# Batch 1's queries turned in full 128x128 transposes, two K^T V products joined into one stretch, and q's transposing transfers issued sooner

## The chip, the cores and the metric

One core of a Trainium2 chip. The metric is the device time of one execution in microseconds (us); a time is quoted as the median of the runs of a kernel. PE is the matrix engine, PEld its weight loads, VectorE (DVE), ScalarE (ACT) and GpSimd (POOL) the others, SP the queue that issues stores and transposing transfers.

## The reference, cut to what matters

```python
kv  = einsum('bhsd,bhse->bhde', k, v)        # 8 batches, 8 heads, 576 rows, 64 wide
out = einsum('bhsd,bhde->bhse', q, kv)       # the "scores" of the kernel
x   = out / sqrt(mean(out*out) + 1e-6) * g_norm       # -> 4608 x 512
h   = x @ w_in                                # 512 -> 2048
y   = elu(h) @ w_out                          # 2048 -> 512
```

## The kernel before: the parts concerned

Each of eight batches gives a group T of 512 rows (a ninth group takes the left-over rows). In a group, PE runs the first layer of batch T (`mm1`, eight steps i, `h_ps`), the second layer of batch T-1 (`mm2`, `o_ps`), and the attention of batch T+1 (K^T V, then scores, tiles named `at` and `se_ps`). From batch 3 on, q is turned by a transposing transfer on the SP queue. Batch 1 has no time for that and is turned on PE:

```python
def q_t_single(q_pk, qt_ps, r, p):            # 32 transposes, 64 columns of q each
    for j in range(J):
        for l in range(2):
            nc.tensor.transpose(qt_ps[l * 64 : l * 64 + 64, r, j * P : j * P + P],
                                q_pk[:, 2 * p + l, j, :], ident)
...
for j in range(J):                            # stage A: mm2 of batch 0 around batch 1
    mm2_quarter(0, j, 0)
    if j == 2: at["q"]()                      # transposes, two ACT copies to qT
for j in range(J):
    mm2_quarter(0, j, 1)
    if j == 1: at["kvu0"]()                   # first half of K^T V
    if j == 2: at["seu0"](scores); at["sq0"](); at["sum0"]()
at["inv0"](); at["mulu0"]()
for j in range(J):
    mm2(0, j, 8, 10)
    if j == 2: at["kvu1"]()                   # second half
at["seu1"](); at["sq1"](); at["sum1"]()
for j in range(J):
    mm2(0, j, 10, 12)                         # w_out's columns 10 to 12
    if j == 1: at["inv1"](); at["xu0"](scores[:, 0, :])
at["mulu1"]()
...                                           # later "xu1": transposes of x, second half
# end of a group T:  if T + 2 < NT: ahead["qd"]()     # q's transposing transfer
# start of a group:  at["landed"]()                   # GpSimd waits for that transfer
#                    fetch(T + 2)                     # then issues q, k, v of batch T+2
# in a group:        if at and i == 0: at["kv"]()     # K^T V of batch T+1
```

## Time and profile before

| | before |
|---|---|
| time, median of the first 3 runs (range) | 284.09 us (283.82 to 284.26) |
| PE busy, share of the span of 282.0 us | 98% |
| start of stage A (first `o_ps` matmul) | 28.31 us |
| stage A (to the first matmul of batch 1's first layer, which writes `at`) | 17.75 us |
| from start of A to the last five output pieces | 235.95 us |

The stages are read off PE's timeline; its starts are 0.17 us ahead of those in the chain of waits, which counts from when the engine is free. The chain and the list of PE's waits are shown in the prediction below. What it only tells is how one sees, in GpSimd's timeline, when transfers end. Columns: start, length, engine, line, operation, and in brackets how long the engine had stood idle and what ended that.

```profile
31.55 0.71 POOL L142 DMA_DIRECT2D w_out_sb<-in_moe_w_out_dram  x1 [1.80 <-DMA w_out_sb<-in_moe_w_out_dram]
33.01 0.74 POOL L104 DMA_DIRECT2D q_pk<-in_q_dram  x1 [0.74 <-DMA k_pk<-in_k_dram]
34.48 0.74 POOL L104 DMA_DIRECT2D q_pk<-in_q_dram  x1 [0.73 <-DMA v_pk<-in_v_dram]
...
37.41 0.74 POOL L118 DMA_DIRECT2D v_pk<-in_v_dram  x1 [0.68 <-DMA k_pk<-in_k_dram]
```

Each issue is held until an older transfer of the same queue has ended, so the brackets name a sequence of endings, one every 1.45 us or so.

### The profile page before, as it was taken

The numbers are of one execution on the slowest core, as the hardware profiler recorded it, in microseconds if no ns is written. First come the engines' busy times: TensorE is split into PE (matmuls) and PEld (weight loads), VectorE is DVE, ScalarE is ACT, GpSimd is POOL, SyncE is SP. The second block draws the span as 40 slices with busy tenths as digits, with TensorE's granted clock in tenths as the row PEclk, the third lists the DMA queues.
The fourth block names the chain that finished last, engine by engine and source line by source line (L and its number), as shares of the span: only waits on it lengthen the run. The fifth ranks groups of instructions, "written<-read, shape, count | busy, mean of one in ns | idle before, by whom it ended". The sixth has DMA issues, their size and how long they took to land.

```text
span 282.0 us, 5163 instructions
## 1 busy us (share of the span) xinstructions
PE 276.0 (98%) x2134; PEld 129.8 (46%) x2134; DVE 159.8 (57%) x232; ACT 153.8 (55%) x221; POOL 56.2 (20%) x98
## 2 busy tenths in 40 slices
PE   7899999999999999999999999999999999999994
PEld 3444544445444444444444444444444444444444
DVE  2559453888388546843693469445854586444400
ACT  2679546666487438533863377337923692333311
POOL 7854422143421341004110421012000000000000
PEclk9999999999999999999999999999999999999999
DMA  7999999697796696359935795455236123010122
GB/s 196 199 200 202 208 201 191 179 170 128 178 177 114 157 157 156 74 149 121 198 78 148 95 211 73 130 114 148 55 94 76 77 38 112 0 77 0 74 76 74
DMA packets 57579, 35.98 MB, mean 128 GB/s; under 512 B 32852, under 2 KB 55124, under 8 KB 57556
## 3 DMA queue, kind: packets, MB, share of 16 engines
q0 software_dynamic: 21808, 17.30, 41.2%
q1 hardware_dynamic: 35348, 17.83, 24.7%
q10 hardware_dynamic: 400, 0.52, 0.6%
q8 instruction: 16, 0.26, 0.4%
q14 instruction: 7, 0.06, 0.1%
HBM read 36.70 MB, written 9.44 MB: 164 GB/s over the span
## 4 chain that ended last, share of the span: by engine, by line
PE 94%; DMA 2%; ACT 1%; DVE 0%; issue 0%; POOL 0%; POOLq 0%
PE h_ps L467 42%; PE o_ps L514 39%; PE o_ps L924 5%; DMA v_pk<-in_v_dram 2%; PE at L174 2%; PE at L467 1%; PE bank L684 1%; PE at L201 1%; PE h_ps L684 1%; PE se_ps L201 1%; ACT r L669 0%; ACT r L672 0%; PE at L185 0%; ACT sq L663 0%; PE se_ps L413 0%
## 5 line engine op out<-in xcount | busy, mean ns | idle before, releaser
L467 PE MATMUL h_ps<-xT,w_in_sb 128*128 128x512 bf16 x536 | 125.7, 379 | 0.0
L514 PE MATMUL o_ps<-w_out_sb,gT 128*128 128x512 bf16 x512 | 120.5, 379 | 0.0
L479 ACT ACTIVATE elu_e<-h_ps 128x1024 bf16<-128x1024 f32 (+1 forms) x71 | 70.0, 995 | 80.1 <-PE h_ps L467 78.5
L467 PEld LDWEIGHTS <-w_in_sb 128*128 128x128 bf16 x552 | 52.5, 98 | 63.3 <-DVE xT L333 1.7
L514 PEld LDWEIGHTS <-gT 128*128 128x128 bf16 x512 | 49.4, 98 | 58.4
L490 DVE TENSOR_SCALAR elu_e<-elu_e 128x1024 bf16<-128x1024 bf16 (+1 forms) x75 | 31.9, 425 | 73.4 <-ACT elu_e L479 73.4
L498 DVE TENSOR_TENSOR gT<-elu_e,h_ps 128x1024 bf16<-128x1024 bf16 (+1 forms) x51 | 60.1, 1179 | 5.3
L527 ACT COPY o_sb<-o_ps 128x512 f32<-128x512 f32 x32 | 18.6, 586 | 15.5 <-PE o_ps L514 15.5
L218 DVE TENSOR_REDUCE ss<-sq 128x16 f32<-128x1024 bf16 x16 | 19.4, 1218 | 11.1 <-ACT sq L213 10.4
L485 ACT ACTIVATE elu_h<-h_ps 128x1024 bf16<-128x1024 f32 (+1 forms) x20 | 19.5, 990 | 0.0
L150 POOL COPY q_bf<-q_pk 128x512 bf16<-128x512 bf16 x24 | 14.4, 629 | 24.3 <-DMA q_pk<-in_q_dram 24.3
L498 DVE TENSOR_TENSOR gT<-elu_e,elu_h 128x1024 bf16<-128x1024 bf16 x20 | 14.2, 709 | 2.5 <-ACT elu_h L485 1.0
L924 PE MATMUL o_ps<-w_out_sb,gT 128*128 128x512 bf16 (+1 forms) x80 | 14.1, 337 | 0.0
L125 POOL COPY gate<-qT 1x1 bf16<-1x1 bf16 x6 | 1.1, 181 | 58.4 <-DMA qT<-q_bf 58.4
L104 POOL DMA_DIRECT2D q_pk<-in_q_dram x14 | 10.6, 758 | 4.5 <-issue 1.5
L229 DVE TENSOR_TENSOR xs<-at,ss 128x512 bf16<-128x512 f32 x16 | 10.2, 682 | 1.2 <-ACT ss L225 1.2
L924 PEld LDWEIGHTS <-gT 128*128 128x128 bf16 x80 | 7.8, 98 | 6.4 <-DVE gT L498 0.4
L213 ACT ACTIVATE sq<-at 128x1024 bf16<-128x1024 f32 x9 | 9.4, 1043 | 1.6 <-PE at L201 1.0
L118 POOL DMA_DIRECT2D k_pk<-in_k_dram x12 | 8.3, 690 | 3.9 <-DMA w_in_sb<-in_moe_w_in_dram 2.4
L118 POOL DMA_DIRECT2D v_pk<-in_v_dram x12 | 8.2, 683 | 3.2 <-DMA w_out_sb<-in_moe_w_out_dram 1.8
L932 ACT COPY o_last<-o_ps 128x512 f32<-128x512 f32 (+1 forms) x5 | 2.5, 500 | 10.8 <-PE o_ps L924 10.8
L174 PEld LDWEIGHTS <-k_pk 64*64 64x64 bf16 x576 | 6.4, 107 | 4.3 <-issue 4.0
(79 smaller groups left out, 140.7 us busy)
## 6 DMA issues: line engine op xcount, KB each, us to landing
out_dram<-o_sb SPq DMA_DIRECT2D x16, 512.0 KB, 3.3
q_pk<-in_q_dram POOLq DMA_DIRECT2D x14, 256.0 KB, 5.7
k_pk<-in_k_dram POOLq DMA_DIRECT2D x6, 576.0 KB, 8.3
v_pk<-in_v_dram POOLq DMA_DIRECT2D x6, 576.0 KB, 11.6
w_in_sb<-in_moe_w_in_dram POOLq DMA_DIRECT2D x5, 256.0 KB, 7.4
st_q<-in_q_dram SPq DMA_DIRECT2D x2, 512.0 KB, 4.7
w_out_sb<-in_moe_w_out_dram POOLq DMA_DIRECT2D x2, 512.0 KB, 13.9
w_out_sb<-in_moe_w_out_dram POOLq DMA_DIRECT2D x4, 256.0 KB, 12.0
```

Of the source, the lines that this page charges most:

```text
L118: nc.gpsimd.dma_start(out=raw[name, b].rearrange("p h j d -> p h (j d)")[:, hs], in_=in_[:, hs])
L150: eng.tensor_copy(out=out_, in_=in_)
L174: nc.tensor.matmul(kv_ps[l * 64 : l * 64 + 64, s, u * 64 : u * 64 + 64], lhsT=bf["k", T][rows, j, 2 * u + l, :], rhs=bf["v", T][rows, j, 2 ...
L218: nc.vector.reduce_sum(out=ss, in_=sq.rearrange("p c (h e) -> p (c h) e", h=H), axis=AX.X)
L467: nc.tensor.matmul(h_ps[a][:, cs], lhsT=w_in_sb[:, c, f * P : f * P + P], rhs=x(c, cs), start=(c == 0), stop=(c == KC - 1),)
L479: nc.scalar.activation(e[:, lo:hi, :], ps, AF.Exp)
L485: nc.scalar.activation(h[:, lo:hi, :], ps, AF.Relu)
L490: nc.vector.tensor_scalar(out=e[:, lo:hi, :], in0=e[:, lo:hi, :], scalar1=1.0, scalar2=1.0, op0=ALU.min, op1=ALU.subtract,)
L498: nc.vector.tensor_tensor(out=gT[T][:, 2 * i + lo : 2 * i + hi, :], in0=e[:, lo:hi, :], in1=h, op=ALU.add if relu else ALU.max,)
L514: nc.tensor.matmul(o_ps[T, j], lhsT=gT[T][:, f, j * P : j * P + P], rhs=w_out_sb[:, f, :], start=(f == 0), stop=(f == FC - 1),)
L527: nc.scalar.copy(o_sb[T][:, j % 2, :], o_ps.pop((T, j)))
L924: nc.tensor.matmul(ps, lhsT=gT[B][:, f, j * P : j * P + P], rhs=w_out_sb[:, f, cols], start=(f == 0), stop=(f == FC - 1),)
```

## The change

Its intent: fewer and fuller PE instructions for batch 1's q, one switch in and out of small tiles less, and enough lead for K and V of batch 7 that the joint product can run a group early. The core of the diff:

```diff
-    def q_t_single(q_pk, qt_ps, r, p):  ... 32 half-width transposes
+    def q_t_single(qb, qt_ps, p):
+        for j in range(J):
+            nc.tensor.transpose(qt_ps[:, p, j * P : j * P + P],
+                qb[:, j, 2 * p : 2 * p + 2, :].rearrange("p h d -> p (h d)"), ident)
@@ q_t
             nc.scalar.copy(qT[:, 0:2, :], qt_ps[:, 0:2, :])
-            nc.scalar.copy(qT[:, 2:4, :], qt_ps[:, 2:4, :])
+            nc.vector.tensor_copy(out=qT[:, 2:4, :], in_=qt_ps[:, 2:4, :])
@@ stage A
     load_w_out(10, 12)
+    unpack_q(1, Q, gated=False)               # four GpSimd copies, repacking q of batch 1
     load_w_out(12, 14)
@@
         mm2_quarter(0, j, 0)
-        if j == 2:
-            at["q"]()
+    at["q"]()
@@
         mm2(0, j, 8, 10)
-        if j == 2:
-            at["kvu1"]()
-    at["seu1"](); at["sq1"](); at["sum1"]()
+    at["kvu1"]()
     for j in range(J):
         mm2(0, j, 10, 12)
-        if j == 1:
+        if j == 0:
+            at["seu1"](); at["sq1"](); at["sum1"]()
+        if j == 2:
             at["inv1"](); at["xu0"](scores[:, 0, :])
@@ fetch: for batch 7 k and v ahead of q
@@ groups
-            if at and i == 0:
+            if at and i == 0 and T in (3, 4):
                 at["kv"]()
+            if i == 2 and T == 5:              # K^T V of batches 6 and 7 in one PSUM tile
+                both = at_tile(FP32).rearrange("p (s x) -> p s x", s=2)
+                ...
+            if i == 5 and T + 2 < B:           # was: at the end of the group
+                ahead["qd"]()
```

More of the change, by code (lines that the diff above doesn't have):

```diff
@@ L125, in after, with unpack_q @@
         nc.gpsimd.tensor_copy(out=gate, in_=ap)
-    def unpack_q(b, eng):
+    def unpack_q(b, eng, gated=True):
         t = raw.pop(("q", b))
@@ L130, in unpack_q @@
         for j in range(J):
-            if j == J - 1:
+            if gated and j == J - 1:
                 after(bf["v", b][0:1, 0, 0, 0:1])
@@ L180, in kv_single @@
                     )
-    def q_t_single(q_pk, qt_ps, r, p):
+    def q_t_single(qb, qt_ps, p):
         for j in range(J):
-            for l in range(2):
-                nc.tensor.transpose(
-                    qt_ps[l * 64 : l * 64 + 64, r, j * P : j * P + P],
-                    q_pk[:, 2 * p + l, j, :],
-                    ident,
-                )
+            nc.tensor.transpose(
+                qt_ps[:, p, j * P : j * P + P],
+                qb[:, j, 2 * p : 2 * p + 2, :].rearrange("p h d -> p (h d)"),
+                ident,
+            )
     def se_mm(T, h, qT, banks):
@@ L247, in q_t @@
             for p in range(NPAIR):
-                q_t_single(raw["q", T], qt_ps, p, p)
+                q_t_single(bf["q", T], qt_ps, p)
             nc.scalar.copy(qT[:, 0:2, :], qt_ps[:, 0:2, :])
-            nc.scalar.copy(qT[:, 2:4, :], qt_ps[:, 2:4, :])
+            nc.vector.tensor_copy(out=qT[:, 2:4, :], in_=qt_ps[:, 2:4, :])
         def q_dma():
@@ L355, in kv_out, with kv_in @@
             )
+        def kv_in(home):
+            st["kv"] = home
+            for u in range(2):
+                kv_single(T, home, u)
         def kv_u(u):
@@ L426, in x_u @@
             return turn
-        pieces = {"kv": kv_all, "q": q_t, "qd": q_dma, "se": se}
+        pieces = {"kv": kv_all, "kvin": kv_in, "kvout": lambda: kv_out(slice(0, 2)), "q": q_t, "qd": q_dma, "se": se}
         pieces["landed"] = lambda: after(st["at"])
@@ L799 @@
         mm2(0, j, 8, 10)
-        if j == 2:
-            at["kvu1"]()
-    at["seu1"]()
-    at["sq1"]()
-    at["sum1"]()
+    at["kvu1"]()
     for j in range(J):
         mm2(0, j, 10, 12)
-        if j == 1:
+        if j == 0:
+            at["seu1"]()
+            at["sq1"]()
+            at["sum1"]()
+        if j == 2:
             at["inv1"]()
@@ L823, in fetch @@
         if b < B:
-            fetch_packed_q(b)
             packed_kv(b)
+            if b < 7:
+                fetch_packed_q(b)
             for name in "kv":
                 fetch_packed_kv(name, b)
+            if b == 7:
+                fetch_packed_q(b)
             unpack_q(b, Q)
@@ L850, in group @@
                     at["kv"]()
+                if i == 5:
+                    ahead["qd"]()
                 if i in (1, 3):
@@ L870, in group @@
             rest()
-            if at and i == 0:
+            if at and i == 0 and T in (3, 4):
                 at["kv"]()
+            if i == 2 and T == 5:
+                both = at_tile(FP32).rearrange("p (s x) -> p s x", s=2)
+                for n, a in enumerate((at, ahead)):
+                    a["kvin"](both[:, :, n * P : n * P + P])
+                for a in (at, ahead):
+                    a["kvout"]()
+            if i == 5 and T + 2 < B:
+                ahead["qd"]()
             if at and i > 5:
@@ L914 @@
         group(T, at, lead, second, {2: (1, 2, 4, 5), B: ()}.get(T, (4, 5)))
-        if T + 2 < NT:
+        if T + 2 == B:
             ahead["qd"]()
```

## The prediction

> **What bounds the kernel now.** I read the page's busy table first, then the list of waits of PE, then the chain of waits in order of time, and last the timelines of GpSimd and of the SP queue.
>
> ```profile
> span 282.0 us, 5163 instructions
> PE 276.0 (98%) x2134; PEld 129.8 (46%) x2134; DVE 159.8 (57%) x232; ACT 153.8 (55%) x221; POOL 56.2 (20%) x98
> ...
> PE bank L603 <- DVE zeros L579: 1.5, 1, 1.5
> PE bank L666 <- ACT sq L663: 0.4, 2, 0.2
> PE kv_ps L174 <- DMA v_pk<-in_v_dram: 0.2, 1, 0.2
> ```
>
> PE is busy 98% of the span, and the three PE lines are the whole list of what PE ever waited for: 2.1 us, all in the first 14 us, which the change does not touch. No other engine is above 57%. From 28 us on, where the change lies, PE has no wait at all. So the time can fall only by what is taken out of PE's own stream, and can rise by any wait that is put into it. The next fence is the chain of waits in order of time (start, length, what), first where batch 1's attention lies inside the second matmul of batch 0, then around one later K^T V.
>
> ```profile
> 28.48 2.59 PE o_ps L514 x12
> 31.07 1.01 PE at L185 x32
> 32.08 2.70 PE o_ps L514 x12
> 34.77 0.41 PE at L174 x36
> 35.18 0.97 PE o_ps L514 x4
> 36.15 0.34 PE se_ps L373 x16
> 36.49 2.27 PE o_ps L514 x10
> 38.76 0.41 PE at L174 x36
> 39.16 0.54 PE o_ps L514 x2
> 39.70 0.34 PE at L373 x16
> 40.04 0.97 PE o_ps L514 x4
> 41.01 0.45 PE se_ps L413 x8
> 41.46 3.02 PE o_ps L514 x14
> ...
> 155.31 0.71 PE at L174 x72
> 156.01 1.83 PE h_ps L467 x8
> 157.84 1.73 PE o_ps L514 x8
> ```
>
> The reader is to see two prices. Twelve plain matmuls take 2.59 us (0.216 each), but 2.70 after the 32 half-width transposes; eight take 1.73, but 1.83 after a K^T V. So PE pays about 0.10 us on leaving a stretch of small tiles. K^T V of 36 matmuls takes 0.41 and of 72 takes 0.71: 0.0083 us each and 0.11 fixed, which is the price on entering. After the eight full 128x128 transposes (L413, 0.45 us, 0.056 each) the fourteen matmuls take 3.02 = 14 x 0.216: no price there.
>
> **What the Trainium skill says.** "TensorEngine Tiling (Array Packing)", section Tiling Modes, Key Properties: changing the tiling mode drains TensorE, changing only the tile does not. The trace agrees: 0.10 to 0.11 us at each edge of a 64-wide stretch and none around the full transposes. "TensorE: Matmul & The Clock Gate", section "Wait — 56ns, not 53.3ns?": at full clock a matmul of N columns takes N/2.4 GHz plus about 2.5 ns, 55.6 ns at 128 and 215.7 at 512; the trace has 0.45/8 = 56 ns and 1.73/8 = 216 ns. "GPSIMD Engine Reference", section 1, Specifications: GpSimd shares its SBUF interfaces with VectorE and is contended by VectorE instructions with two SBUF inputs or in a two-port mode. In this trace three of its q copies take 1.73 us in most batches and 1.92 us in two of them, one with VectorE work beside it; that is compatible, no more. No page gives a landing time for the transfers that matter below; the trace does.
>
> **The change part by part.**
> 1. *Full transposes of batch 1's q.* Removed: 32 half-width transposes, 1.01 us, and the 0.11 us paid after them. Added: 16 full ones, at the measured 0.056 us each 0.90 us, with no price behind. Gain 1.12 - 0.90 = 0.22 us, all on PE's path. The price of it lies off PE: four GpSimd copies of q (about 0.58 us apart) and one of the two qT copies goes from ACT (1.02 us) to VectorE, which is idle from 31.3 to 37.6 us in the timeline.
> 2. *K^T V of batches 6 and 7 in one stretch.* Before: twice 0.71 + 0.10 = 1.62 us. After: 0.11 + 144 x 0.0083 + 0.10 = 1.41 us. Gain 0.21 us, or about 0.20, one pair of edges.
> 3. *The second K^T V of batch 1 and its scores later.* As many PE instructions and as many edges as before; the order alone changes. PE gain 0. It matters for waits (rivals below).
> 4. *q's transposing transfers sooner.* They are on the SP queue, not on PE. They went out at 122.05, 151.19 and 180.32 us, though the x transposes in front of them had been issued by 116.4, 145.6 and 174.7; GpSimd then waited for them before it fetched the next batch (58.4 us of waits in all, none of it on PE's path). Going out at step 5 they run some 5.6 us earlier and so does the next fetch. Gain on the path 0; it is what makes part 2 possible, as K and V of batch 7 are now needed a group sooner.
>
> Sum without new waits: 0.22 + 0.20 = 0.42 us of 284.09, so 283.67 us.
>
> **The rivals.**
> *A, no new wait:* 283.67. For it: PE has no waits in these stretches today, and every order in the kernel seems tuned to that.
>
> *B, PE waits for w_out's columns 10 to 12.* Before, they are first used at 40.04. After: 16 matmuls (28.48 + 3.46 = 31.94), transposes to 32.84, 8 matmuls to 34.57, then 0.41 + 0.97 + 0.34 to 36.29, 12 matmuls with their edge 2.70 to 38.99, the second K^T V to 39.40: they are used there, 0.64 us sooner. When do they land? GpSimd, when it issues, waits for older transfers of its queue, so its timeline shows their ends: first halves of K and V of batch 1 at 33.0 and 34.5, w_out 8 to 10 at 36.0, second half of K at 37.4, 1.45 us apart. The transfer engines run at 200 GB/s throughout. Going on so (an estimate from these steps), the second half of V lands at 38.7 and w_out 10 to 12 near 39.9, just in time before and about 0.5 us too late after. Against it: 39.9 is an extrapolation, 40.04 is only an upper bound, and the 16 transfer engines need not finish in order. I give it one chance in two. Cost 0.3 to 0.5 us, so that the time stays near 284.1.
>
> *C, GpSimd copies q of batch 1 too late.* The second half of that q lands at about 29.0 (GpSimd's issue of w_out at 29.06 was held for it). Four copies at 0.58 end near 31.4; with VectorE's two-input work at 30.1 to 31.3 beside them perhaps 31.7. The transposes start at 31.94 after the move behind the fourth quarter (they would have started at 31.07 before it). So a slack of 0.2 to 0.5 us; one chance in four of a wait up to 0.2 us. The two w_out issues behind the copies go out up to 2.4 us later, but some 10 us of transfers are queued in front of them, so their landing should not move.
>
> *D, the second half of batch 1's x comes late.* Scores of the second half end at 40.28 instead of 40.04, and from there to the scaled rows it takes 44.27 - 40.04 = 4.23 us (square 1.02, sum 1.22, Ln and Exp 0.55, scaling 1.29, with their gaps). That is 44.5, against 44.3 at which PE comes to the transposes. Only the second four of them need the last row, 0.22 us later, so 0 to 0.15 us.
>
> *E, K and V of batch 7 are not there.* q of batch 6 goes out at about 145.6 and takes the 4.5 us it took before (151.19 to 155.72), so K and V of 7, now ahead of q, are issued by 150.6 and 151.4. Before, q, K and V (1.66 MB) plus a 0.5 MB store took from 157 to 170.7 us. K and V with the store are three quarters of that, some 9 to 10 us, so 161 to 162. PE needs batch 7 at 162.9 (163.02 less the 0.81 of the K^T V that left the front of the group, plus 0.7 for batch 6). One chance in six of a wait, of up to 1 us. The PSUM tile that both products share is copied out twice (0.37 us each), while PE has 1.8 us of matmul before it needs the tile again: free.
>
> **Range and chances.** 0.42 us gained, less about 0.20 for B (half a chance of 0.4), 0.03 for C, 0.03 for D and 0.08 for E leaves 0.08; but the waits overlap (one in C or D shortens B), and the ones that I found are the ones such a change was presumably arranged around, so I take 0.24 and predict 283.85 us. The three runs before spread over 0.44 us. With all of A and a low draw 283.3; with B and E 284.5. Two per cent are 5.7 us: PE would have to lose or gain a fifth of a whole group's 29 us, and no step does that.
>
> **What would show it.** Part 1: transposes x16 near 0.90 us with 0.216 us matmuls behind them. Part 2: one stretch x144 near 1.3 us in the group of 151 to 181 us, one group later none. Part 4: GpSimd's wait for qT down from 13 to 16 us a group to about 8 to 10. B: a PE wait, or a hole in the chain, at the first use of w_out after the second K^T V; C: one in front of the transposes; D: one in front of the second transposes of x; E: PE waiting for k_pk or v_pk near 163 us. The prediction is wrong if PE shows waits over 1 us in all, or if the stretches cost PE more than their counts say.

## The result, and the profile after

The changed kernel took 284.15 us (median of 4, 283.76 to 284.47), the kernel before 284.15 us on the same occasion (4 runs): ratio 1.0001, 95% interval 0.9984 to 1.0019. The ratio is the mean time of one kernel's fast runs over that of the other's of the same rounds, so not quite the ratio of the medians. A gain of 0.42 us would be 0.15%, which this interval cannot exclude; the traces decide. They show the forecast saving of PE work, and show it spent again: from the start of A to the last pieces the two traces of the changed kernel are 0.17 and 0.19 us longer than the two of the kernel before.

The page after, and the list of PE's waits:

```profile
span 282.7 us, 5105 instructions
PE 273.6 (97%) x2088; PEld 129.7 (46%) x2118; DVE 161.5 (57%) x233; ACT 152.8 (54%) x220; POOL 59.6 (21%) x102
...
PE kv_ps L174 <- DMA v_pk<-in_v_dram: 0.6, 2, 0.4
PE h_ps L688 <- DMA w_in_sb<-in_moe_w_in_dram: 0.4, 1, 0.4
...
PE o_ps L518 <- issue: 0.3, 2, 0.2
```

Two cautions for the reader. This profiled run was the slowest of its four (284.47), and its head before stage A, which the change does not touch, is 0.57 us longer than in the trace before: the waits for v and w_in above are all there. And the trace has 46 PE matmuls fewer than before though only 16 were removed, so some records are missing; holes of 0.05 us called "issue" in the chain are such. Neither says anything of the change. The chain of waits in the stages that it does touch:

```profile
32.50 0.91 PE at L184 x16
33.41 0.02 issue
33.43 1.02 ACT qT L248
34.45 0.02 issue
34.47 0.70 DVE qT L249
35.17 0.04 issue
35.22 0.48 PE at L174 x36
...
42.40 2.59 PE o_ps L518 x12
44.99 0.68 PE se_ps L417 x8
...
163.16 1.31 PE at L174 x144
164.47 1.83 PE h_ps L471 x8
```

The transposes x16 take 0.91 us and the joint stretch x144 takes 1.31 us with 0.10 behind it: both as forecast. But between transposes and K^T V the chain now runs through ACT and DVE. The second copy of qT did not run beside the first one, it ran after it, and K^T V had to wait for the PSUM tile that both read (the kernel has one buffer for it). VectorE's timeline names ACT's copy as what it waited for; why it did is not shown, as the two copies touch different halves of their tiles. And the second transposes of x, 0.45 us before, take 0.68. A third loss lies at the end of the third group. VectorE scales the last part of x, PE's next weights wait for that, and in VectorE's and GpSimd's timelines of the changed kernel one finds

```profile
121.70 1.48 POOL L104 DMA_DIRECT2D q_pk<-in_q_dram  x2
123.16 0.76 POOL L118 DMA_DIRECT2D k_pk<-in_k_dram  x1
...
122.85 0.58 DVE L332 TENSOR_SCALAR xT<-xT,g_col 128x1024 bf16<-128x1024 bf16 x1
```

In the kernel before it is

```profile
122.01 0.48 DVE L333 TENSOR_SCALAR xT<-xT,g_col 128x1024 bf16<-128x1024 bf16 x1
```

and GpSimd did not issue until 127.06 there. The Trainium skill, "SBUF — State Buffer", section "SBUF: two separate sides", says that VectorE, in a two-port mode, and GpSimd share an exclusive pair of ports and that the loser is blocked; the longer scaling beside an issue agrees with that, though no view shows in which mode the scaling ran.

### The profile page after: what moved, and what is told of

It is laid out like the page before. It is cut to its first block, busy times and chain, and to the rows that moved or that the text cites. A ratio compares the mean times of both kernels' runs of the same rounds, so it can differ in the third digit from the quotient of the medians.

```text
span 282.7 us, 5105 instructions
## 1 busy us (share of the span) xinstructions
PE 273.6 (97%) x2088; PEld 129.7 (46%) x2118; DVE 161.5 (57%) x233; ACT 152.8 (54%) x220; POOL 59.6 (21%) x102
## 4 chain that ended last, share of the span: by engine, by line
PE 89%; DMA 5%; ACT 2%; DVE 1%; issue 1%; POOL 0%; POOLq 0%
PE h_ps L471 40%; PE o_ps L518 37%; PE o_ps L941 5%; DMA w_in_sb<-in_moe_w_in_dram 3%; DMA k_pk<-in_k_dram 2%; PE at L174 2%; PE bank L688 1%; PE at L471 1%; PE at L200 1%; PE se_ps L200 1%; DVE xs L228 0%; DVE ss L217 0%; PE se_ps L417 0%; ACT elu_e L483 0%; ACT qT L248 0%
## 5 line engine op out<-in xcount | busy, mean ns | idle before, releaser
L518 PE MATMUL o_ps<-w_out_sb,gT 128*128 128x512 bf16 x488 | 117.9, 379 | 1.4 <-issue 0.3
L494 DVE TENSOR_SCALAR elu_e<-elu_e 128x1024 bf16<-128x1024 bf16 (+1 forms) x75 | 32.5, 433 | 73.2 <-ACT elu_e L483 73.1
L531 ACT COPY o_sb<-o_ps 128x512 f32<-128x512 f32 x32 | 18.6, 585 | 15.3 <-PE o_ps L518 14.7
L150 POOL COPY q_bf<-q_pk 128x512 bf16<-128x512 bf16 x28 | 17.3, 650 | 32.9 <-DMA q_pk<-in_q_dram 32.9
```

The costliest lines, as they stand in the source:

```text
L150: eng.tensor_copy(out=out_, in_=in_)
L494: nc.vector.tensor_scalar(out=e[:, lo:hi, :], in0=e[:, lo:hi, :], scalar1=1.0, scalar2=1.0, op0=ALU.min, op1=ALU.subtract,)
L518: nc.tensor.matmul(o_ps[T, j], lhsT=gT[T][:, f, j * P : j * P + P], rhs=w_out_sb[:, f, :], start=(f == 0), stop=(f == FC - 1),)
L531: nc.scalar.copy(o_sb[T][:, j % 2, :], o_ps.pop((T, j)))
```

## The experiments

Eleven runs were made, of six new kernels and five repeats, on three occasions, each with its own runs of the kernel before. Each new kernel is given as an edit of the kernel before or of the changed one. The table has the stages of every trace. A is stage A. "Group 3 to 4" is the distance between the scores of batch 4 and of batch 5 on PE; "joint" is the sum of the three such distances after it, in which the K^T V of batches 6 and 7 lie; "A to last" runs from the start of A to the last five output pieces. Left out is the stretch from the end of A to the scores of batch 4: it is 60.24 to 60.26 us in eleven traces, 60.35 in the first one before and 60.45 in the first one after.

| kernel | A starts | A | A ends | group 3 to 4 | joint | A to last |
|---|---|---|---|---|---|---|
| before | 28.31 | 17.75 | 46.06 | 29.14 | 86.60 | 235.95 |
| b2 | 28.32 | 17.75 | 46.07 | 29.14 | 86.60 | 235.84 |
| after | 28.88 | 17.92 | 46.80 | 29.25 | 86.39 | 236.12 |
| a2 | 28.50 | 18.00 | 46.50 | 29.27 | 86.39 | 236.03 |
| e_kv | 28.39 | 17.75 | 46.14 | 29.27 | 87.15 | 236.54 |
| e_kv2 | 28.38 | 17.74 | 46.12 | 29.26 | 86.93 | 236.31 |
| e_q | 28.67 | 17.97 | 46.64 | 29.14 | 86.60 | 236.08 |
| f_both | 28.57 | 17.63 | 46.20 | 29.31 | 86.40 | 235.70 |
| f_both2 | 28.04 | 18.33 | 46.37 | 29.36 | 86.38 | 236.44 |
| f_best | 28.24 | 18.05 | 46.29 | 29.14 | 86.39 | 235.94 |
| f_best2 | 28.81 | 17.53 | 46.34 | 29.14 | 86.38 | 235.42 |
| f_old3 | 28.66 | 17.70 | 46.36 | 29.14 | 86.38 | 235.59 |
| e_noqd | 28.87 | 17.75 | 46.62 | 29.14 | 90.12 | 239.36 |

**b2: the kernel before again.** No edit.

> The kernel before, unchanged, profiled a second time: how much do stages of the same program differ from run to run? Stage A (from the first second-layer matmul to the first first-layer matmul of batch 1) was 17.74 us in the first trace, the two groups in which K^T V of batches 6 and 7 lie were 58.28 us together, and everything from the start of A to the last five output pieces 235.95 us. My theory: each of these three repeats within 0.1 us, and what differs between runs is the head before A (28.48 us in the first trace), which waits for transfers. Rival: the stages themselves wander by several tenths, and then no difference of that size between one trace of each kernel means anything.

All its stages repeated within 0.11 us. A difference of 0.2 us in a stage can be read, if a second trace shows it too.

**a2: the changed kernel again.** No edit.

> The changed kernel, unchanged, profiled a second time and timed in five rounds. In its first trace stage A was 17.91 us instead of 17.52 (0.22 less than before, as forecast), with a late K^T V behind the two copies of qT (0.1) and a wait of 0.23 at the second transposes of x; the two groups were 58.07. My theory: both waits are there again, A within 0.1 of 17.91, the groups at 58.07, the sum from A to the last pieces 235.9 to 236.2, and the ratio within 0.1% of 1. Rival: the first trace was unlucky, A falls to about 17.55, and the kernel is 0.15% faster.

Both waits came again, A was 18.00, and five more rounds gave 284.12 us against 284.15: ratio 1.0005 (0.9985 to 1.0024). The first trace was not unlucky. A is 0.10 above the 17.90 that the two waits account for, and 0.07 in e_q below; this is taken up under f_best2.

**e_kv: the late parts alone.** The changed kernel with its edits to batch 1 taken back.

```diff
 (before)
+  joint K^T V of batches 6 and 7, k and v ahead of q for batch 7, qd at i == 5
```

> The kernel before with the later parts of the change alone: K^T V of batches 6 and 7 in one stretch, K and V of batch 7 fetched ahead of q, q's transposing transfers at step 5 of a group. My theory: stage A as in the kernel before, 17.74; the two groups 58.07, that is 0.21 less; the time 0.2 us (0.07%) below the kernel before, unless the sooner fetch disturbs VectorE at a group's end (0.1 in the first trace of the changed kernel). Rival: the sooner transfers cost PE as much as the stretch saves, and nothing is left.

A stayed at 17.75 and group 3 to 4 lost 0.13, so that loss belongs to the sooner transfers. But the joint groups were 0.55 us longer, not 0.21 shorter, and the time was 284.31 against 284.15: ratio 1.0009 (0.9990 to 1.0027). The chain of waits of this trace:

```profile
165.60 0.34 PE at L201 x16
165.94 0.06 PE se_ps L201 x4
166.00 0.46 issue
166.45 0.35 PE se_ps L201 x12
```

In the middle of the scores behind the joint stretch PE stood still with nothing to wait for.

**e_kv2: the same once more.**

> The late parts alone, profiled again. In its first trace PE stood 0.46 us within the scores behind the joint stretch with nothing to wait for, and lost 0.63 there in all, so that the groups were 0.5 us longer, not 0.21 shorter. My theory: that was a single hiccup (the changed kernel has the same stretch and did not show it in two traces); here from A to the last pieces it is 235.85 (0.21 gained, 0.11 to 0.24 lost to VectorE's slower scaling). Rival: it comes again, and is a price of 144 small matmuls in a row.

My theory fell: the pause came again, at the same instruction of the 32 weight loads, 0.36 us this time, and the joint groups were 86.93. (Its single timed run, 285.12 us, is the longest of this kernel's, but its span on the chip, 282.4, is not.) It is not simply a price of the stretch either, as none of the seven traces of the changed kernel and its variants has it, though their stretch is the same and their PE program only 32 instructions shorter up to there. What it is stays open; e_noqd below, the same PE program with a wait of 2 us just ahead of the stretch's second half, has no pause.

**e_q: the early parts alone.**

```diff
 (before)
+  repacked q, full transposes, at["q"] after the quarter, second K^T V and scores later
```

> The kernel before with the early parts alone: full transposes of batch 1's q from the repacked copy, second K^T V and scores later. My theory: transposes 0.9 us instead of 1.0, no price behind them, and yet stage A 17.9 us, as K^T V waits 0.1 us for the two copies of qT, which run one after the other, and the second transposes of x wait 0.2 us; the two groups 58.28 as before; the time 0.1 to 0.2 us above the kernel before, at most even. Rival: the early parts alone gain their 0.22 us, A is 17.5, and the loss comes from the later parts.

As expected: A 17.97, group 3 to 4 at 29.14, joint 86.60, time 284.21 against 284.15, ratio 1.0008 (0.9991 to 1.0025). So the early parts lose their own gain within stage A.

**e_noqd: the joint stretch without the sooner transfers.** e_kv with `qd` back at the end of the group.

```diff
-                if i == 5: ahead["qd"]()
-            if i == 5 and T + 2 < B: ahead["qd"]()
-        if T + 2 == B: ahead["qd"]()
+        if T + 2 < NT: ahead["qd"]()
```

> The kernel before with the joint K^T V and K, V ahead of q for batch 7, but q's transposing transfers at the old place. My theory: the sooner transfers gain nothing by themselves and are what the joint stretch needs: K and V are issued at about 156 instead of 152, V lands at 164 to 167 against a need at 162.9, so PE waits 1 to 4 us for v_pk there and the time is 0.5 to 1.3% above the kernel before. Rival: V lands within 7 us of its issue, and the joint stretch would have done without the sooner transfers.

287.39 us against 283.89, ratio 1.0117 (1.0101 to 1.0133): the only clear difference. V of batch 7 was issued at 157.44 and landed 7.85 us later, PE waited 2.0 us for it, and group 3 to 4 was back at 29.14. So part 4 is what the joint stretch stands on. The table of windows (first the window, its length and PE's busy time, near the end the granted clock) shows why 2.0 us of waiting cost 3.7:

```profile
161.00:163.30 2.30, 2.30 (x80) 1.26 (x79) 1.16 (x2) 1.59 (x2) 0.00 (x0) 1.00 1.21 207
163.30:165.30 2.00, 0.08 (x10) 0.00 (x0) 0.49 (x1) 0.00 (x0) 0.00 (x0) 1.00 1.27 201
165.30:167.30 2.00, 1.97 (x75) 1.26 (x75) 0.00 (x0) 0.65 (x2) 0.00 (x0) 0.60 1.29 151
167.30:169.30 2.00, 2.00 (x6) 0.61 (x4) 0.00 (x0) 0.00 (x0) 0.00 (x0) 0.55 1.08 310
169.30:171.30 2.00, 2.00 (x40) 1.13 (x39) 0.57 (x2) 1.73 (x3) 0.27 (x1) 1.00 0.08 19
```

After the idle stretch the clock was granted at little over half for 4 us; eight matmuls that take 1.83 us took 3.24.

**f_both: the two waits of stage A taken away.** On the changed kernel:

```diff
-            nc.scalar.copy(qT[:, 0:2, :], qt_ps[:, 0:2, :])
+            nc.vector.tensor_copy(out=qT[:, 0:2, :], in_=qt_ps[:, 0:2, :])
@@ mm2(0, j, 14, FC, ...)
-        if j == 0:
+        if j == 1:
             at["xu1"](scores[:, 1, :])
```

> The changed kernel with its two waits in stage A taken away: both copies of qT on VectorE (0.70 us each, so both done in 1.4 instead of 1.72 us), and the second transposes of x two matmuls later. My theory: stage A falls from 17.92 and 18.00 to 17.55, the 0.22 us of the full transposes then showing; groups 5 and 6 stay 0.21 below the kernel before; from A to the last pieces 235.6 to 235.75 instead of 236.03 to 236.12. Rival: PE then waits for w_out or for the second half of x's transposed rows instead, and A stays at 17.8 or more. The timed ratio cannot tell 0.15% and should read same.

A fell to 17.63, and the transposes of x took 0.45 us again. The chain goes through w_out's columns 10 to 12 here, landed at 39.64 and used at 39.69, which is where the 0.10 above 17.53 lies. Yet it was timed at 284.58 against 283.89, ratio 1.0023 (1.0010 to 1.0036): slower by its interval. Its profiled run was the fastest of its six.

**f_best: and the fetch behind the scaling of x.** On f_both:

```diff
         if T + 2 < NT:
+            if 2 < T < 6:
+                after(xT[T](0, None)[0:1, J - 1, 0:1])
             at["landed"]()
```

> As the run before, and GpSimd issues the next batch's fetch only after VectorE has scaled the last part of x at a group's end. My theory: the 0.11 us that the third group lost (VectorE's scaling 0.58 to 0.61 us instead of 0.48 while GpSimd issued) is gone, its distance from score to score back at 29.14; from A to the last pieces 235.5, which is 0.4 less than the kernel before. Rival: the later fetch brings K and V of batch 7 too late for the joint stretch, and PE waits there.

VectorE's scaling was back at 0.48 us and group 3 to 4 at 29.14: the third loss comes from the fetch, by what in it is not shown. 283.75 us against 283.89, ratio 0.9998 (0.9985 to 1.0010). But A was 18.05, and the list of PE's waits and the chain say why:

```profile
PE o_ps L518 <- DMA w_out_sb<-in_moe_w_out_dram: 0.5, 1, 0.5
...
27.11 12.62 DMA w_out_sb<-in_moe_w_out_dram
39.73 0.04 issue
39.77 0.59 PE o_ps L518 x2
```

PE stood for w_out's columns 10 to 12, which landed at 39.73. This is rival B of the prediction, which the list of waits of the changed kernel had not shown.

**f_best2 and f_both2: the same two again.**

> f_best again, the same kernel. Its first trace had a wait of 0.5 us for w_out in stage A (18.05 us). My theory: how long PE waits depends on how early the head ends: about 39.75 less the time at which A begins less 11.0, so 0.5 at 28.24 and none at 28.8; A plus its beginning is 46.2 to 46.4 again. Rival: the wait was an accident of one run, A is 17.55.

> f_both again, the same kernel, for one more trace. It was timed 0.2% slower than the kernel before, yet its trace gave 235.70 us from A to the last pieces, 0.2 less; its profiled run was the fastest of its six, and after the last first-layer matmul VectorE stood 0.46 us between two instructions with nothing to wait for, 0.3 us on the path. Theory: the stages repeat (A 17.6 to 18.0, with the beginning of A to 46.2 to 46.4), and the time that is missing lies in the head and in that pause. Rival: a stage is longer in other runs than the first trace showed.

The account holds. Without other waits PE comes to w_out 10 to 12 some 11.1 us after A starts (in the prediction 39.40 - 28.48, plus the 0.17 between the two views). For f_best2 that is 39.9, after the landing (11.9 us after the issue at 27.91): no wait, and A is 17.53. For f_both2 it is 39.1: a wait of 0.8 in its list, and A is 18.33. An early head is taken back, and whatever the start, A ends at 46.20 to 46.37 in all four traces. f_best2 is also the trace in which the forecast stands as it was made, transposes, the matmuls behind them at full speed, and no wait:

```profile
32.43 0.89 PE at L184 x16
33.32 1.73 PE o_ps L518 x8
35.05 0.41 PE at L174 x36
...
42.17 3.02 PE o_ps L518 x14
45.20 0.45 PE se_ps L417 x8
```

17.75 - 0.22 = 17.53.

`prof <label> --tile w_out_sb`, with a window around the issue of columns 10 to 12, gives the time from that issue to its landing in every trace. In the eight traces with the issue at 27.59 or later it is 11.9 to 12.1 us; in the five with an earlier issue (f_best, a2, e_q, f_old3, f_both2, from 27.11 to 27.53) it is 12.3 to 12.8. In f_best V's second half, just ahead in the queue, landed at 37.7 (25.78 + 11.9) and w_out 2.0 us behind it; in the trace after it was 38.5 and 1.3 us. So in these five the early head brought the queue forward, but not this transfer. All five are kernels with the four repacking copies of q right behind the issue, and no kernel without them had so early an issue: whether the copies or the early issue delay it is not shown. It also explains most of the odd tenth in a2 and e_q: in a2 PE begins on these columns at 39.76, as they land (27.37 + 12.3).

In three rounds f_best2 took 283.86 us against 283.92, ratio 0.9996 (0.9981 to 1.0012). That f_both is timed slower is only partly explained: its traces lose 0.17 and 0.22 in group 3 to 4 and have, at the very end, a pause of VectorE of 0.46 us with nothing to wait for, 0.3 on the path, both times; the rest was in runs that were not profiled.

**f_old3: f_best with batch 1's second half at its old place.**

```diff
         mm2(0, j, 8, 10)
-    at["kvu1"]()
+        if j == 2: at["kvu1"]()
+    at["seu1"](); at["sq1"](); at["sum1"]()          # as before the change; xu1 at j == 0
```

> Full transposes, joint K^T V, sooner q, both copies of qT on VectorE, the fetch behind the scaling of x, and the second K^T V and its scores of batch 1 back at their old place (so without the reordering of batch 1's second half). The last runs showed PE waiting up to 0.5 us for w_out's columns 10 to 12, which land near 39.7 us whatever PE does; the reordering uses them 0.6 us sooner than the kernel before. My theory: with the old order they are used some 0.4 us later than in f_best, stage A is 17.53 (up to 0.15 more if the second half of V of batch 1 is then what PE waits for), and from A to the last pieces it is 235.4 to 235.6, 0.3 to 0.5 below the kernel before; the timed ratio reads 0.998 to 0.9995. Rival: any order of this stage ends when the transfers allow it, near 46.1 us of the span, and A is again 17.75 or more.

283.67 us against 283.92, ratio 0.9986 (0.9972 to 1.0001): the best of all, not quite clear of 1 by its interval. A was 17.70, not 17.53, as w_out landed at 40.25 in this run, 12.8 us after its issue and half a microsecond later than in f_best. A ended at 46.36. So the rival given with it has a point: this stage ends when the transfers let it.

## Why the prediction was right or wrong

The time, 284.15 us, lies in the range, 0.30 above the predicted 283.85, and the change stayed within 2%, as forecast. That is worth little: the range, 283.3 to 284.5, holds anything from a gain of 0.8 us to a loss of 0.4. The gain of 0.24 itself did not come. By its own steps:

- *PE bounds, so only its own stream and new waits count.* Right.
- *Part 1, gain 0.22.* Right in size: 16 transposes 0.89 to 0.91 us (0.90 forecast), eight matmuls behind them 1.73. It shows in full only in f_best2, where A is 17.53.
- *Part 2, gain 0.21.* Right: 1.31 + 0.10 = 1.41 us; 86.39 against 86.60 in both traces of the changed kernel.
- *Part 1's cost, "one of the two qT copies goes from ACT (1.02 us) to VectorE".* This is the first step that failed. I took it for a relief. The two copies ran one after the other, 1.02 + 0.70 us, and since PE came sooner, K^T V was late: 0.14 us (K^T V done at 35.69 in the chain, against 29.05 + 3.46 + 0.90 + 1.73 + 0.41 = 35.55). No rival named it. Before, the two ACT copies were done at 34.05, with 0.7 us to spare.
- *D, the second half of x.* The mechanism was right, the size was off: 0.23 us measured (0.68 against 0.45) where I gave 0 to 0.15 and an expectation of 0.03. The chain from scores to scaled rows was as long as I had it (40.98 to 45.21). But the rows go into PE as weights, and I had taken the time of the matmul for the time of need: the fifth weight load began at 45.27, right behind the scaling, and its transpose only after that. With 17.53 + 0.14 + 0.23 = 17.90, stage A (17.92) is accounted for; a2 and e_q have up to 0.10 more, most of it B.
- *Part 4, "gain on the path 0".* Wrong by 0.11 us. GpSimd's fetch now falls into VectorE's scaling of x at a group's end. It came in all six traces with the sooner transfers and the fetch right behind them, in none without them, and went in the three in which the fetch was put behind the scaling. The sign that I gave for this part did not come: GpSimd's waits for qT were 11.8, 15.3 and 12.6 us, where they had been 15.7, 13.4 and 13.4, and not 8 to 10. The transfers do go out sooner, at 117.35, 147.36 and 176.34.
- *B, w_out late.* Right as a mechanism: a landing near 39.9 was estimated, and 39.64 to 39.81 in three traces, 40.25 in one, was measured. In the trace before it landed at 39.8 (27.74 + 12.1), 0.25 ahead of its use. The first trace of the changed kernel does not show the wait, because its head was late (A at 28.88) and the copies delayed PE by 0.14 more; f_best2 has none either, with a head as late and no wait for copies. With an earlier head B appears: about 0.1 us in a2, 0.5 and 0.8 in f_best and f_both2.
- *C.* Did not come: the four copies ended at 31.54, PE began the transposes at 32.50.
- *E.* Did not come, but not by much: V of batch 7, issued at 152.97, landed 9.5 us later (the tile view of v_pk), near 162.4, and PE came to batch 7 near 163.8 (163.16 and half of the stretch). In e_noqd it took 7.85 us.
- *The sum.* 0.42 gained; 0.14 + 0.23 + 0.11 = 0.48 lost, which leaves the traces 0.06 worse; they read 0.17 and 0.19 worse (236.12 and 236.03 against 235.95 and 235.84). The rest is the stretch left out of the table in the first pair (0.10), which did not come again, and w_out in the second (about 0.1). My own reckoning had left 0.08 of gain. I then took 0.24, on the thought that the waits I had found were arranged around. That choice was the wrong one.

## What to carry to other kernels

When one engine is busy for 98% of the span, a saving on it is worth only the least slack among the things that feed it; list for each of them when it is ready and when it will now be needed, PSUM tiles that wait for their readers included. Waits in a row hide one another, so that removing the one that a trace shows may only uncover the next, here down to a transfer that landed no sooner when the work ahead of it did. And a transfer that is moved sooner off the path still makes its issuing engine work at another moment: look at what runs there.

## What the Trainium skill lacked or had wrong

- "TensorE: Matmul & The Clock Gate", section "Why this matters for your kernels", advises against PE idle gaps over some 3 us. Here a gap of 2.0 us, after a stretch of 64x64 matmuls, was followed by about 4 us at a granted clock of 0.55 to 0.60, so that it cost 3.7 us.
- "SBUF — State Buffer", section "SBUF: two separate sides", describes the port pair as a lock under which the loser is blocked for a whole instruction. Here VectorE's scaling grew only from 0.48 to between 0.58 and 0.70 us beside GpSimd issues of 0.75 us each; if the lock is what delayed it, it was not held for a whole issue.
- No page that I found gives how long a GpSimd-issued transfer takes when others are queued ahead of it, which set the end of stage A: w_out's columns 10 to 12 landed 11.9 to 12.8 us after their issue.
- None explains the pauses without a wait that came twice at the same instruction of one program: 0.36 and 0.46 us on PE (e_kv), 0.46 us on VectorE (f_both).
